# Sigmoid attention with a routed block: values with v as the stationary operand, four heads per step

## The chip, the core and the metric

The kernel runs on one core of a Trainium2 chip. The metric is the device time of one execution in microseconds. TensorE does the matmuls, VectorE and ScalarE the elementwise work, GpSimd the rest; SyncE (SP) and GpSimd issue the DMAs.

## The reference

Shapes: 8 batches, 12 heads, 448 tokens, 64 features per head, all float32; model width D = 12 x 64 = 768, hidden width 1024, capacity 128.

```
scores = q @ k.T / sqrt(64) - log(448)
attn   = 1 / (1 + exp(-scores))
x      = (attn @ v), heads side by side: (8, 448, 768)
per batch b:
  s   = x[b] @ w_gate                      # (448,)
  top = the 128 tokens with the largest s
  h   = relu(x[b, top] @ w1); ye = h @ w2
  out[b] = x[b]; out[b, top] += sigmoid(s[top])[:, None] * ye
```

## The kernel before, in words

Work goes by pairs of heads: 48 pairs, six per batch. `load` (L65 to L76) brings q, k and v of two pairs in three DMAs of 448 KB on the SP queue, tokens on 112 partitions, four consecutive tokens per partition, two loads ahead. `transposes` (L121) lets GpSimd put the two heads of a pair side by side (L128), turns the four 112-token chunks of q and of k on TensorE against an identity (L132) into a PSUM buffer of the pool `ps_1`, and VectorE copies them out (L137), so that the 64 features of each head lie on partitions.

`scores` (L140) makes one chunk of 112 keys for both heads: two matmuls of 64 rows, 448 query columns (L146), one head in partitions 0 to 63, the other in 64 to 127; ScalarE then takes one sigmoid over 896 elements per partition out of a `ps_sc` buffer (two of them) into the attention tile (L152). `values` (L157) makes 112 query rows of the output for both heads: for each head four matmuls that accumulate over the key chunks, with a 112x112 block of attention as the stationary operand and 64 columns of v streaming (L167). After the fourth chunk VectorE copies the pair's 112x512 result into x_b, the batch's 112x4x768 tile (L174).

The main loop (L303) interleaves by hand: for each chunk c, scores of pair i, then values of pair i - 1; after chunk 1 the transposes of pair i + 1; after chunks 1 and 3 one piece of the routed block of an earlier batch (`step`). The pieces of the routed block are: `store_and_gate` (x_b to out by one DMA on SP, the gate's dot products on VectorE, L187, a diagonal on GpSimd), `rank` (the gates of all tokens to all partitions by a matmul with ones, L200 and L202; VectorE counts for every token how many rank above it, L212, and builds one-hot columns, L218), `select` (eight narrow matmul passes per batch for index and gate, L226), `gather` (the 128 chosen rows, turned, as matmuls of x_b with the one-hot columns, L242), `ffn1` (two parts of 4 x 6 matmuls, L256, and a relu on ScalarE), `ffn2` (two parts of 8 matmuls of 384 columns, L268, times the gate on VectorE, L270), and `scatter` (an indirect DMA on GpSimd that adds the rows to out, L273). All PSUM tiles of the routed block and the transposes share the two `ps_1` buffers; x_b has two buffers. Each engine runs its instructions in program order, and the order above is the program order.

Of the kernel before, what the change touches and what calls it, by code (L numbers as in the profile page):

```python
# [16 lines left out]
def kernel(  # L17
# [17 lines left out]
    P = 128  # L35
    CP = 112            # tokens on the partitions: token p * NCH + c is row p of chunk c
    NCH = S // CP
    NPAIR = H // 2
    GP = 2              # head pairs per load
    NG = NPAIR // GP  # L40
# [3 lines left out]
    N = B * NPAIR  # L44
# [3 lines left out]
    PSUM = bass.MemoryType.PSUM  # L48
    assert S == NCH * CP and D == KD * P and F == KF * P and KF % 4 == 0 and 0 < CAP < S
# [4 lines left out]
    raw = ctx.enter_context(tc.tile_pool(name="raw", bufs=3))  # L54
# [8 lines left out]
    raws = {}  # L63

    def load(gi):  # L65
        b, g = divmod(gi, NG)
        h0, nh = 2 * GP * g, 2 * GP
        tiles = []
        for nm, src in (("q", q), ("k", k), ("v", v)):
            t = raw.tile([CP, nh, NCH, Dh], F32, name=f"raw_{nm}")  # L70
            nc.sync.dma_start(
                out=t.rearrange("p h c d -> p h (c d)"),
                in_=src[b, h0:h0 + nh].rearrange("h (p c) d -> p h (c d)", c=NCH),
            )
            tiles.append(t)
        raws[gi] = tiles  # L76
# [3 lines left out]

    iden = const.tile([P, P], F32, name="iden")
    make_identity(nc, iden)
    bias_s = const.tile([P, 1], F32, name="bias_s")
    nc.vector.memset(bias_s, NEG_LOG_S)

# [5 lines left out]
    # earlier[p, c, t]: 1 where position t of the row lies before token (c, p)  # L91
# [3 lines left out]
    # [..., 0] the token's number in its sequence, [..., 1] its gate score  # L95
    tok_gate = [const.tile([CP, NCH, 2], F32, name=f"tok_gate{n}") for n in range(2)]

    def late_consts():
# [5 lines left out]
        for w, src in ((w1_sb, moe_w1), (w2_sb, moe_w2)):  # L104
            nc.gpsimd.dma_start(out=w, in_=src.rearrange("(t p) f -> p t f", p=P))
# [4 lines left out]
        for t in tok_gate:  # L110
            nc.gpsimd.iota(t[:, :, 0], pattern=[[1, NCH]], base=0,
                           channel_multiplier=NCH, allow_small_or_imprecise_dtypes=True)
# [6 lines left out]
    qkT, attn = {}, {}  # L119

    def transposes(i):  # L121
        b, hp = divmod(i, NPAIR)
        g, gi = divmod(hp, GP)
        tiles = raws[b * NG + g]
        qkT[i] = head.tile([P, 2, NCH, CP], F32, name="qkT")
        for a in range(2):
            pairs = head.tile([CP, NCH, 2, Dh], F32, name=f"pairs{a}")
            nc.gpsimd.tensor_copy(  # L128
                pairs, tiles[a][:, 2 * gi:2 * gi + 2].rearrange("p j c d -> p c j d"))
            ptr = ps_1.tile([P, 512], F32, name="ps1")  # L130
            for c in range(NCH):
                nc.tensor.transpose(  # L132
                    ptr[:, c * CP:(c + 1) * CP],
                    pairs[:, c].rearrange("p j d -> p (j d)"),
                    iden[:CP, :CP],
                )
            nc.vector.tensor_copy(  # L137
                qkT[i][:, a], ptr[:, :S].rearrange("e (c p) -> e c p", c=NCH))

    def scores(i, c):  # L140
        t = qkT[i]
        if c == 0:
            attn[i] = head.tile([CP, 2, NCH, S], F32, name="attnT")
        psc = ps_sc.tile([P, 2, 512], F32, name="psc")
        for j in range(2):
            nc.tensor.matmul(  # L146
                psc[:CP, j, :S],
                t[j * Dh:(j + 1) * Dh, 1, c, :],
                t[j * Dh:(j + 1) * Dh, 0].rearrange("e c p -> e (c p)"),
                start=True, stop=True,  # L150
            )
        nc.scalar.activation(attn[i][:, :, c, :], psc[:CP, :, :S], AF.Sigmoid,  # L152
                             bias=bias_s[:CP], scale=QK_SCALE)

    x_tiles, pav = {}, {}

    def values(i, m):  # L157
        b, hp = divmod(i, NPAIR)
        g, gi = divmod(hp, GP)
        vt = raws[b * NG + g][2]  # L160
        if m == 0:
            pav[i] = ps_o.tile([P, NCH, 2, Dh], F32, name="pav")
            if hp == 0:
                x_tiles[b] = xp.tile([CP, NCH, D], F32, name="x_b")
        for j in range(2):
            for c in range(NCH):
                nc.tensor.matmul(  # L167
                    pav[i][:CP, m, j, :],
                    attn[i][:, j, c, m * CP:(m + 1) * CP],
                    vt[:, 2 * gi + j, c, :],  # L170
                    start=(c == 0), stop=(c == NCH - 1),
                )
        if m == NCH - 1:
            nc.vector.tensor_copy(  # L174
                x_tiles[b][:, :, 2 * hp * Dh:2 * (hp + 1) * Dh],
                pav.pop(i)[:CP].rearrange("p c j d -> p c (j d)"))
# [171 lines left out]
```

## Time and profile before

| | us |
|---|---|
| median of three runs | 848.65 |
| the three runs | 847.45, 848.65, 849.12 |
| span of the profiled execution, first to last instruction | 846.6 |
| TensorE (PE) busy in it | 815.3 |
| PE weight loads (PEld), beside PE | 610.0 |
| ScalarE busy | 205.3 |
| VectorE (DVE) busy | 195.5 |
| GpSimd (POOL) busy | 84.8 |

The profile is of one execution, on the only core. Busy times of engines overlap one another. A matmul's record contains its way through the array, so records of consecutive matmuls overlap, and the distance of their starts, or the chain of work that ended last, shows what one costs. Each fp32 matmul stands there as two weight loads and two MATMUL records.

### The profile page before, as it was taken

To read this page: it belongs to the slowest core of one execution; us is meant where nothing else is said; L and a number is where in the kernel's file an instruction comes from. 1 tells how busy PE (TensorE), PEld (TensorE's weight loads), DVE (VectorE), ACT (ScalarE), POOL (GpSimd) and SP (SyncE) were. 2 spreads that over 40 slices of the span, in tenths; PEclk is the share of its full clock that TensorE was granted. 3 is DMA by queue.
4 is the path that set the end of the run, shared out by engine and by line. 5 is a ranking of instruction groups with operands and counts; after the bars stand their busy time and mean duration, and the time that the engine had idled before them with its cause. 6 is when DMAs were issued, how large, how long until landed. Compare 5 with 4: busy or idle time off the path is not lost.

```text
span 846.6 us, 12702 instructions
## 1 busy us (share of the span) xinstructions
PE 815.3 (96%) x5728; PEld 610.0 (72%) x5728; DVE 195.5 (23%) x425; ACT 205.3 (24%) x217; POOL 84.8 (10%) x131
## 2 busy tenths in 40 slices
PE   6999999999999999999999999999999999999586
PEld 4677787677876778677786778767787677876484
DVE  0211601134101341113401143011611125101420
ACT  2433311232122321233121331213311232112000
POOL 5111100101001100011000110011100111000000
PEclk9999999999999999999899999999999999999778
DMA  9952310331003410124101232032320201001101
GB/s 279 314 120 60 107 48 1 85 115 60 23 1 84 130 45 23 42 43 131 44 22 44 41 132 66 1 63 54 102 65 1 41 11 77 2 1 19 65 1 19
DMA packets 37030, 54.64 MB, mean 65 GB/s; under 512 B 1456, under 2 KB 33712, under 8 KB 36080
## 3 DMA queue, kind: packets, MB, share of 16 engines
q1 hardware_dynamic: 34432, 44.05, 17.9%
q0 software_dynamic: 2544, 9.78, 4.9%
q8 instruction: 45, 0.74, 0.4%
q14 instruction: 9, 0.07, 0.0%
HBM read 39.67 MB, written 14.16 MB: 64 GB/s over the span
## 4 chain that ended last, share of the span: by engine, by line
PE 91%; issue 5%; DVE 2%; DMA 1%; ACT 0%; POOLq 0%; POOL 0%
PE pav L167 39%; PE psc L146 23%; PE ps L256 9%; PE ps L268 9%; PE ps L242 6%; PE ps L132 4%; PE ps L226 1%; DMA out_dram<-x_b 1%; PE ps L200 1%; DVE qkT L137 1%; DVE junk L212 1%; DMA raw_q<-in_q_dram 0%; ACT attnT L152 0%; DVE sel L218 0%; POOLq L343 0%
## 5 line engine op out<-in xcount | busy, mean ns | idle before, releaser
L167 PEld LDWEIGHTS pav<-raw_v,attnT 112*112 112x112 f32 x3072 | 317.5, 178 | 118.9 <-issue 118.3
L167 PE MATMUL pav<-raw_v,attnT 112*112 112x64 f32 x3072 | 345.4, 265 | 0.4 <-ACT attnT L152 0.4
L152 ACT ACTIVATE attnT<-psc,bias_s 112x896 f32<-112x896 f32 x192 | 193.1, 1007 | 467.2 <-PE psc L146 467.2
L146 PE MATMUL psc<-qkT 64*112 64x448 f32 x768 | 217.1, 589 | 1.0 <-DVE qkT L137 0.7
L137 DVE COPY qkT<-ps 128x448 f32<-128x448 f32 x96 | 56.2, 619 | 213.0 <-PE ps L132 213.0
L174 DVE COPY x_b<-pav 112x512 f32<-112x512 f32 x48 | 33.2, 692 | 261.5 <-PE pav L167 261.5
L256 PEld LDWEIGHTS ps<-xeT,w_sb 128*128 128x128 f32 x768 | 87.0, 192 | 4.8 <-DVE qkT L137 4.7
L256 PE MATMUL ps<-xeT,w_sb 128*128 128x128 f32 x768 | 89.5, 277 | 0.0
L268 PE MATMUL ps<-w_sb,hT 128*128 128x384 f32 x256 | 86.1, 490 | 0.0
L146 PEld LDWEIGHTS psc<-qkT 64*112 64x112 f32 x768 | 59.2, 173 | 30.7 <-issue 8.9
L128 POOL COPY pairs<-raw_q 112x512 f32<-112x512 f32 x48 | 29.5, 614 | 516.3 <-PE ps L132 449.9
L268 PEld LDWEIGHTS ps<-w_sb,hT 128*128 128x128 f32 x256 | 47.4, 190 | 34.6 <-DVE qkT L137 4.7
L242 PEld LDWEIGHTS ps<-sel,x_b 112*128 112x128 f32 x384 | 54.7, 232 | 5.9 <-issue 5.9
L242 PE MATMUL ps<-sel,x_b 112*128 112x128 f32 x384 | 56.4, 318 | 0.0
L132 PE MATMUL ps<-iden,pairs 112*128 112x112 f32 x384 | 47.8, 264 | 6.6 <-POOL pairs L128 6.0
L132 PEld LDWEIGHTS ps<-iden,pairs 112*128 112x128 f32 x384 | 40.0, 148 | 12.5 <-POOL pairs L128 7.1
L258 ACT ACTIVATE hT<-ps 128x512 f32<-128x512 f32 x16 | 9.6, 597 | 116.4 <-PE ps L256 116.4
L128 POOL COPY pairs<-raw_k 112x512 f32<-112x512 f32 x48 | 29.7, 619 | 15.5 <-DMA raw_k<-in_k_dram 9.4
L187 DVE CUSTOM_DVE_ANT_0 junk<-x_b,wg_b 112x768 f32<-112x768 f32 x32 | 30.6, 958 | 2.1 <-DVE x_b L174 0.5
L270 DVE TENSOR_SCALAR oe<-ps,gate 128x384 f32<-128x384 f32 x16 | 9.9, 618 | 90.9 <-PE ps L268 90.9
L273 POOL DMA_INDIRECT out_dram<-oe,idx x8 | 12.9, 1608 | 133.7 <-DVE oe L270 95.9
L245 DVE COPY xeT<-ps 128x384 f32<-128x384 f32 x16 | 8.9, 558 | 61.7 <-PE ps L242 61.7
(33 smaller groups left out, 121.8 us busy)
## 6 DMA issues: line engine op xcount, KB each, us to landing
raw_q<-in_q_dram SPq DMA_DIRECT2D x24, 448.0 KB, 4.0
raw_k<-in_k_dram SPq DMA_DIRECT2D x24, 448.0 KB, 4.9
raw_v<-in_v_dram SPq DMA_DIRECT2D x24, 448.0 KB, 3.9
out_dram<-x_b SPq DMA_DIRECT2D x8, 1344.0 KB, 6.6
w_sb<-in_moe_w_dram POOLq DMA_DIRECT2D x2, 3072.0 KB, 23.6
wg_b<-in_moe_w_gate_dram POOLq DMA_DIRECT2D x1, 336.0 KB, 6.7
out_dram<-oe,idx POOLq DMA_INDIRECT x8, 5.6
```

The source lines that it names most:

```text
L128: nc.gpsimd.tensor_copy(pairs, tiles[a][:, 2 * gi:2 * gi + 2].rearrange("p j c d -> p c j d"))
L132: nc.tensor.transpose(ptr[:, c * CP:(c + 1) * CP], pairs[:, c].rearrange("p j d -> p (j d)"), iden[:CP, :CP],)
L137: nc.vector.tensor_copy(qkT[i][:, a], ptr[:, :S].rearrange("e (c p) -> e c p", c=NCH))
L146: nc.tensor.matmul(psc[:CP, j, :S], t[j * Dh:(j + 1) * Dh, 1, c, :], t[j * Dh:(j + 1) * Dh, 0].rearrange("e c p -> e (c p)"), start=True, ...
L152: nc.scalar.activation(attn[i][:, :, c, :], psc[:CP, :, :S], AF.Sigmoid, bias=bias_s[:CP], scale=QK_SCALE)
L167: nc.tensor.matmul(pav[i][:CP, m, j, :], attn[i][:, j, c, m * CP:(m + 1) * CP], vt[:, 2 * gi + j, c, :], start=(c == 0), stop=(c == NCH - 1),)
L174: nc.vector.tensor_copy(x_tiles[b][:, :, 2 * hp * Dh:2 * (hp + 1) * Dh], pav.pop(i)[:CP].rearrange("p c j d -> p c (j d)"))
L187: nc.vector.tensor_tensor_reduce(out=junk, in0=x_b[:, c, :], in1=wg_b, scale=1.0, scalar=0.0, op0=ALU.mult, op1=ALU.add, accum_out=tg[:, c ...
L242: nc.tensor.matmul(ps[:, t - t0, :n], x_b[:, c, t * P:(t + 1) * P], sel[:, c, s0:s0 + n], start=(c == 0), stop=(c == NCH - 1))
L256: nc.tensor.matmul(ps[:, f, :n], w1_sb[:, t, fc * P:(fc + 1) * P], xeT[:, t, :n], start=(t == 0), stop=(t == KD - 1))
L268: nc.tensor.matmul(ps[:n, :ND], hT[:, t, :n], w2_sb[:, t, cols], start=(t == 0), stop=(t == KF - 1))
L273: nc.gpsimd.indirect_dma_start(out=out_flat[:, :], out_offset=bass.IndirectOffsetOnAxis(ap=st[b]["idx"][:n, 0:1], axis=0), in_=st[b]["oe"] ...
```

## The change

A step now holds four heads (24 steps, three per batch). What it does:

- `load`: q and k are read in eight DMAs of 32 partitions each, per tensor four: head of the pair (j) and half of the features (e) choose the partitions, token t x 14 + r is row r of partition t, and each partition reads one run of 864 floats (13 tokens of 64 and 32 floats) for two heads. v comes in four DMAs of 32 partitions with three tokens (768 bytes) per run, and the remaining half chunk in four DMAs with one token (256 bytes) per run. 16 DMAs per step, two steps ahead; q and k tiles have two buffers, v tiles three.
- `turn`: four VectorE 32x32 transposes per step (384, 384, 128 and 896 elements per lane) give kT and qT with features on partitions; the TensorE transposes and GpSimd copies of q and k are gone.
- `scores`: seven chunks per step: six of 128 keys for a pair of heads, and one that holds the half chunks (64 keys) of both pairs. One sigmoid each.
- `values`: v is stationary (64 columns), 448 columns of attention stream; the two heads of a pair write partitions 0 to 63 and 64 to 127 of one PSUM tile. First the half chunks (64 rows) of all four heads, then three chunks of 128. The result is x^T; VectorE copies it to xT, and `back` turns it with four TensorE transposes per pair into a `ps_1` buffer and copies that to x_b.
- `store_and_gate` stores x a second time, to a DRAM tile x_d; `select` fetches the 128 rows from x_d with an indirect DMA, and `turn_rows` turns them with six TensorE transposes per batch in two halves. The matmul `gather` is gone. `ffn2` adds the row, and `scatter` writes without addition.
- `ps_1` has one buffer, the layers have their own PSUM pool `ps_f` with one; x_b has one buffer.
- Order: in step i the chunks 0 to 3, slot 2i, the chunks 4 to 6, turn of step i + 1, loads of step i + 2, slot 2i + 1, values of step i. A slot holds first `back` (of step i - 1), then pieces of the routed block by a fixed table: for batch b, `store_and_gate` in slot 6b + 7, `rank` in 6b + 9, `select` in 6b + 11, `turn_rows` in 6b + 12 and 6b + 13, two of the eight `ffn1` pieces in each of 6b + 13 to 6b + 16, `ffn2` in 6b + 17 and 6b + 18, `scatter` in 6b + 18. The weights are loaded after the first four chunks of step 0. What remains after slot 47 runs behind the last step.

The diff's core:

```diff
-    xp = ctx.enter_context(tc.tile_pool(name="xp", bufs=2))
-    moe = ctx.enter_context(tc.tile_pool(name="moe", bufs=2))
+    moe = ctx.enter_context(tc.tile_pool(name="moe", bufs=1))
-    ps_1 = ctx.enter_context(tc.tile_pool(name="ps_1", bufs=2, space=PSUM))
+    ps_f = ctx.enter_context(tc.tile_pool(name="ps_f", bufs=1, space=PSUM))
+    ps_1 = ctx.enter_context(tc.tile_pool(name="ps_1", bufs=1, space=PSUM))
...
+            t = raw.tile([P, 2, TB * Dh], F32, name=f"raw_{nm}")
+            for j in range(2):
+                for e in range(2):
+                    p0 = (2 * j + e) * TT
+                    nc.sync.dma_start(
+                        out=t[p0:p0 + TT, :, 0:RUN],
+                        in_=bass.AP(
+                            tensor=src.tensor,
+                            offset=src.offset + (b * H + h0 + j) * S * Dh + e * TT,
+                            ap=[[TB * Dh, TT], [2 * S * Dh, 2], [1, RUN]]),
+                    )
...
+    def turn(i):
+        kT[i] = head.tile([P, 2, TB, TT], F32, name="kT")
+        src = raws[i][0].rearrange("p a (r d) -> p a r d", d=Dh)
+        for pr in range(2):
+            nc.vector.transpose(
+                kT[i][:, pr, :4 * NF],
+                src[:, pr, :4 * NF, 0:TT].rearrange("p (m c) d -> p c m d", c=NF))
+        nc.vector.transpose(kT[i][:, :, 4 * NF:], src[:, :, 4 * NF:, 0:TT])
+        qT[i] = head.tile([P, 2, TB, TT], F32, name="qT")
+        src = raws[i][1].rearrange("p a (r d) -> p a r d", d=Dh)
+        nc.vector.transpose(qT[i], src[:, :, :, 0:TT])
...
+        parts = [(pr, slice(4 * NF, TB), pr * Dh, Dh) for pr in range(2)]
+        if n < 2 * NF:
+            parts = [(n // NF, slice(4 * (n % NF), 4 * (n % NF) + 4), 0, P)]
+        for pr, rows, p0, np_ in parts:
+            for j in range(2):
+                d = slice(j * Dh, (j + 1) * Dh)
+                nc.tensor.matmul(
+                    psc[p0:p0 + np_, j, :S],
+                    kT[i][d, pr, rows, :].rearrange("e r t -> e (r t)"),
+                    qT[i][d, pr].rearrange("e r t -> e (r t)"),
+                    start=True, stop=True)
...
+    def values(i):
+        tv, th = raws[i][2:]
+        out_t = [ps_o.tile([P, S], F32, name="pav") for _ in range(2)]
+        for pr in range(2):
+            for j in range(2):
+                p = slice(pr * Dh, (pr + 1) * Dh)
+                nc.tensor.matmul(out_t[pr][j * Dh:(j + 1) * Dh], th[p, j, :],
+                                 attn[i][p, 2 * NF, j, :], start=True, stop=False)
+        xT[i] = head.tile([P, 2, S], F32, name="xT")
+        for pr in range(2):
+            for c in range(NF):
+                for j in range(2):
+                    nc.tensor.matmul(
+                        out_t[pr][j * Dh:(j + 1) * Dh],
+                        tv[:, 2 * pr + j, c * Dh:(c + 1) * Dh],
+                        attn[i][:, pr * NF + c, j, :],
+                        start=False, stop=(c == NF - 1))
             nc.vector.tensor_copy(
+                xT[i][:, pr].rearrange("p (t r) -> p r t", r=TB),
+                out_t[pr].rearrange("p (r t) -> p r t", t=TT))
...
+    def back(i, pr):
...
+        ps = ps_1.tile([P, NCH, P], F32, name="ps1")
+        for c in range(NCH):
+            nc.tensor.transpose(ps[:CP, c, :], xT[i][:, pr, c * CP:(c + 1) * CP], iden)
+        hp = 2 * g + pr
+        nc.vector.tensor_copy(x_tiles[b][:, :, hp * P:(hp + 1) * P], ps[:CP])
...
+        xe = moe.tile([P, D], F32, name="xe", bufs=2)
+        nc.gpsimd.indirect_dma_start(
+            out=xe[:n], out_offset=None, in_=st[b]["x_d"][:, :],
+            in_offset=bass.IndirectOffsetOnAxis(ap=row[:n, 0:1], axis=0))
...
+    def turn_rows(b, n, half):
+        if half == 0:
+            st[b]["xeT"] = moe.tile([P, KD, P], F32, name="xeT")
+        ps = ps_1.tile([P, 4, P], F32, name="ps1")
+        for t in range(3):
+            tt = half * 3 + t
+            nc.tensor.transpose(ps[:, t, :n], st[b]["xe"][:n, tt * P:(tt + 1) * P],
+                                iden[:n, :n])
+        nc.vector.tensor_copy(st[b]["xeT"][:, half * 3:half * 3 + 3, :n], ps[:, :3, :n])
...
+    for i in range(NI):
+        for n in range(NF + 1):
+            scores(i, n)
+        if i == 0:
+            load_weights()
+        fill(2 * i)
+        for n in range(NF + 1, 2 * NF + 1):
+            scores(i, n)
+        if i + 1 < NI:
+            turn(i + 1)
+        if i + 2 < NI:
+            load(i + 2)
+        fill(2 * i + 1)
+        values(i)
+    for s in range(2 * NI, last + 1):
+        fill(s)
```

## Rows read from the trace of the kernel before

**Rows 1.** The page's busy times: us, share of the span, instructions.

```profile
PE 815.3 (96%) x5728; PEld 610.0 (72%) x5728; DVE 195.5 (23%) x425; ACT 205.3 (24%) x217; POOL 84.8 (10%) x131
```

**Rows 2.** The page's chain that ended last: shares by engine, by line.

```profile
PE 91%; issue 5%; DVE 2%; DMA 1%; ACT 0%; POOLq 0%; POOL 0%
PE pav L167 39%; PE psc L146 23%; PE ps L256 9%; PE ps L268 9%; PE ps L242 6%; PE ps L132 4%; PE ps L226 1%; DMA out_dram<-x_b 1%; PE ps L200 1%; DVE qkT L137 1%; DVE junk L212 1%; DMA raw_q<-in_q_dram 0%; ACT attnT L152 0%; DVE sel L218 0%; POOLq L343 0%
```

**Rows 3.** Groups by line and shape: count, busy us, mean ns, idle before.

```profile
L167 PE MATMUL pav<-raw_v,attnT 112*112 112x64 f32 x3072 | 345.4, 265 | 0.4 <-ACT attnT L152 0.4
...
L152 ACT ACTIVATE attnT<-psc,bias_s 112x896 f32<-112x896 f32 x192 | 193.1, 1007 | 467.2 <-PE psc L146 467.2
...
L137 DVE COPY qkT<-ps 128x448 f32<-128x448 f32 x96 | 56.2, 619 | 213.0 <-PE ps L132 213.0
...
L174 DVE COPY x_b<-pav 112x512 f32<-112x512 f32 x48 | 33.2, 692 | 261.5 <-PE pav L167 261.5
```

**Rows 4.** Chain in order of time, 400 to 412 us: start, us, what.

```profile
400.85 0.79 PE ps L200 x2
...
401.75 0.94 PE psc L146 x4
402.69 1.72 PE pav L167 x16
...
407.06 0.41 PE ps L132 x4
```

**Rows 5.** Instructions of L146: shortest, median, longest duration in ns.

```profile
L146 PE MATMUL psc<-qkT x768: 536/627/1086, 8.7 to 783.8; 64*112 64x448 f32 x192
```

**Rows 6.** Waits: who for what, us in total, times, longest.

```profile
PEld pav L167 <- issue: 118.3, 178, 0.7
```

**Rows 7.** Timeline of ScalarE, 12.5 to 15.5 us: start, us, what, idle before.

```profile
13.34 1.91 ACT L152 ACTIVATE attnT<-psc,bias_s 112x896 f32<-112x896 f32 x2 [0.23 <-PE psc L146]
```

**Rows 8.** Timeline of all engines, 400.9 to 405.4 us.

```profile
404.33 1.01 PE L146 MATMUL psc<-qkT 64*112 64x448 f32 x4
...
405.39 1.01 ACT L152 ACTIVATE attnT<-psc,bias_s 112x896 f32<-112x896 f32 x1 [1.58 <-PE psc L146]
```

**Rows 9.** Timeline of the tail behind the last pair, 785 to 850 us.

```profile
800.35 0.40 PE L202 MATMUL ps<-tok_gate,iden 112*112 112x4 f32 x2
...
808.36 1.28 PE L226 MATMUL ps<-tok_gate,sel 112*128 112x2 f32 x6
...
817.35 11.13 PE L256 MATMUL ps<-xeT,w_sb 128*128 128x128 f32 x96
...
828.32 10.49 PE L268 MATMUL ps<-w_sb,hT 128*128 128x384 f32 x32
...
838.84 0.62 DVE L270 TENSOR_SCALAR oe<-ps,gate 128x384 f32<-128x384 f32 x1 [4.47 <-PE ps L268]
839.74 1.57 POOL L273 DMA_INDIRECT out_dram<-oe,idx  x1 [41.07 <-DVE oe L270]
```

**Rows 10.** Timeline of the start, 0 to 9.6 us.

```profile
0.75 0.38 SPq L71 DMA_DIRECT2D raw_q<-in_q_dram  x1
...
8.72 1.09 PE L146 MATMUL psc<-qkT 64*112 64x448 f32 x2 [0.72 <-DVE qkT L137]
```

**Rows 11.** DMA: the queue's packets, MB, share; issues: KB, us to landing.

```profile
q1 hardware_dynamic: 34432, 44.05, 17.9%
...
raw_q<-in_q_dram SPq DMA_DIRECT2D x24, 448.0 KB, 4.0
...
out_dram<-x_b SPq DMA_DIRECT2D x8, 1344.0 KB, 6.6
...
out_dram<-oe,idx POOLq DMA_INDIRECT x8, 5.6
```

**Rows 12.** Second 21.2 us: length, engines' busy us, granted clock, DMA share, GB/s.

```profile
21.20:42.40 21.20, 20.26 (x145) 13.14 (x143) 4.85 (x8) 8.85 (x9) 3.52 (x6) 1.00 1.07 313
```

More of the change, by code (lines that the diff above doesn't have):

```diff
@@ L140, in scores @@
[L140 to L176, printed above, removed]
+    def load_weights():
+        for w, src in ((w1_sb, moe_w1), (w2_sb, moe_w2)):
+            nc.gpsimd.dma_start(out=w, in_=src.rearrange("(t p) f -> p t f", p=P))
@@ L264, in ffn2 @@
         oe = st[b]["oe"]
-        ps = ps_1.tile([P, 512], F32, name="ps1")
+        ps = ps_f.tile([P, 512], F32, name="psf")
         cols = slice(part * ND, (part + 1) * ND)
@@ L275, in scatter, with put @@
             out_offset=bass.IndirectOffsetOnAxis(ap=st[b]["idx"][:n, 0:1], axis=0),
[L276 removed]
+            in_=st[b]["oe"][:n], in_offset=None)
+    places = {}
+    def put(s, fn, *args):
+        places.setdefault(s, []).append((fn, args))
     def routed(b):
[L279 to L280 removed]
+        s = 2 * NQ * (b + 1) + 1
+        put(s, store_and_gate, b)
+        put(s + 2, rank, b)
+        s += 4
         for s0, n in SLOTS:
[L282 to L288 removed]
@@ L291 @@
-    todo = []
-    def step():
-        while todo:
-            try:
-                next(todo[0])
-                return
-            except StopIteration:
-                todo.pop(0)
-    transposes(0)
-    late_consts()
-    for i in range(N + 1):
-        if i < N and i % GP == 0 and i // GP + 2 < B * NG:
-            load(i // GP + 2)
-        for c in range(NCH):
-            if i < N:
-                scores(i, c)
-            if i > 0:
-                values(i - 1, c)
-            if c == 1 and i + 1 < N:
-                transposes(i + 1)
-            if c % 2 == 1:
-                step()
-        if i > 0 and i % NPAIR == 0:
-            todo.append(routed(i // NPAIR - 1))
@@ L317 @@
-    while todo:
-        step()
+            put(s, select, b, s0, n)
+            for half in range(2):
+                put(s + 1 + half, turn_rows, b, n, half)
+            for f in range(KF):
+                put(s + 2 + f // 2, ffn1, b, n, f)
+            for part in range(2):
+                put(s + 2 + KF // 2 + part, ffn2, b, n, part)
+            put(s + 2 + KF // 2 + 1, scatter, b, n)
+            s += 2 + KF // 2 + 2
+    for i in range(NI):
+        put(2 * i + 2, back, i, 0)
+        put(2 * i + 3, back, i, 1)
@@ new lines, with fill @@
+    fills = {s: list(v) for s, v in places.items()}
+    places = {}
+    for b in range(B):
+        routed(b)
+    order = {}
+    last = max(places)
+    for s in range(last + 1):
+        own, rest = fills.get(s, []), places.get(s, [])
+        order[s] = own + rest
+    def fill(s):
+        for fn, args in order.get(s, []):
+            fn(*args)
+    turn(0)
+    late_consts()
+    for i in range(NI):
+        for n in range(NF + 1):
[11 more added lines that the diff above has]
+        values(i)
```

165 lines of the change are left out of this document (80 added, 85 removed).

## The prediction

> **What bounds the kernel now.** I read the busy times first: TensorE is busy 815.3 of 846.6 us, VectorE 195.5 [rows 1]. The chain that ended last says the same from the other side: 91% of it is PE work, 39% the values matmuls of L167, 23% the scores of L146, 9% each the two layers of the routed block, 6% its gather by matmul (L242), 4% the transposes of q and k (L132) [rows 2]. So time is won only where TensorE's own stream gets shorter, and lost where that stream begins to wait.
>
> The stream's unit is the pass: every fp32 matmul stands in the trace as two weight loads and two MATMULs (L167: 48 pairs x 4 chunks x 2 heads x 4 key chunks = 1536 matmuls, 3072 records [rows 3]). Sixteen values passes take 1.72 us [rows 4], 0.107 us each. They stream 64 columns but load 112 stationary columns each; that load is what they cost. The wider passes are set by what streams: 32 passes of 384 columns take 10.49 us [rows 9], 0.328 each, so 448 columns cost 0.328 x 448/384 = 0.38, and L200 has 0.79 for two [rows 4]. A score chunk is four passes of 448 columns, yet takes 0.94 [rows 4]: the two heads sit in different 64-row halves of the array and stream together, 2 x 0.38 = 0.76, and 0.18 is left over. Of that 0.09 is a weight load that nothing covers (passes last 627 or 536 ns [rows 5]); the rest is the change between the half-array and whole-array form, after which L167's loads stand idle 0.7 us, 178 times [rows 6].
>
> **The change, part by part**, for a step of four heads (24 steps; before, two pairs).
>
> *Values.* Before: 128 passes x 0.107 = 13.7 us. After, v is stationary (64 columns) and 448 columns of attention stream. Three full key chunks, two pairs, two heads, two passes: 24 passes, the two heads in the two column halves. If they stream together as the score halves do: 12 x 0.38 = 4.6. The half chunk uses four quarters of the array: 8 passes, 2 x 0.38 = 0.76 if all four overlap. Three changes of form at 0.1 (bounds 0.09 to 0.18 from above): 0.3. Sum 5.65. No row shows a column tile; the far bound is no overlap between the column halves, (24 + 4) x 0.38 + 0.3 = 10.9, the near one 5.65 less the switches, 5.35. I take 5.65, because L146 is the nearest row and its two halves overlap in full.
>
> *Scores.* Seven chunks for eight (the seventh in four quarters, 0.94 too), but in bursts of four and three with nothing between, on the same two PSUM buffers. A sigmoid starts 1.06 us after its chunk [rows 8], lasts 1.007 [rows 3] and two run 1.91 together, 0.905 apart [rows 7]. So the third chunk waits for the first sigmoid: it starts at 2.1, not 1.88, and the bursts cost 4.0 and 3.1, in sum 7.1. Bounds: 7 x 0.76 = 5.3 if PE alone set it, 7 x 1.06 = 7.4. Before it was 8 x 0.94 = 7.5. Almost nothing is won here.
>
> *Turning.* PE transposes of q and k go (16 passes a step, four in 0.41 [rows 4]), with GpSimd's copies and two VectorE copies per pair. Eight transposes bring x^T back: 2 x 0.41 and a change of form, 1.0. VectorE gets four 32x32 turns a step, 1792 elements per lane. No such instruction is in the trace; its copies take 619 ns for 448 elements and 692 for 512 [rows 3], 1.14 ns an element and 0.11 fixed, so 1792 x 1.14 + 4 x 0.11 = 2.5 us. I take that; they hide behind the second score burst and the values (3.1 + 5.65 = 8.8), so even 3.5 times the price costs nothing, and a price of zero gains nothing. VectorE in all: 2.5, two x^T copies 1.3, two x copies 1.4, a third of a batch's gate, rank and rest (some 15 us) 5: 10 us in a step of 14 to 23.
>
> *Routed block.* Its two layers stay: 11.13 and 10.49 a batch [rows 9]. Rank 0.9 stays, select is 8 small passes at 1.28/6 [rows 9], 1.7. The gather's 48 matmul passes go; in their place a row gather by DMA (unseen; bounds: a q load lands in 4.0 us, the scatter in 5.6 [rows 11], plus 1.57 on GpSimd [rows 9], so 4 to 7; I take 7, and one slot of 9 us or more covers it) and six transposes, 0.6. With one ps1 buffer where there were two, the second half of the turned rows follows x^T's transposes at once, and then the first layer waits for its copy: two copies and their hand-over, 1.8 a batch (0 if something hides it, 4 if the later halves wait as well). Batch: 26.6; a step: 8.9. The new token order, L270's added operand, the scatter without addition and the x^T copies (behind the first score burst, 4.0) stay beside TensorE's stream: nothing, except in the tail.
>
> *Loads.* q and k are read twice with overlap: 16 DMAs for 2.23 MB a step where three loads of 0.46 MB stood. SP's issue is 16 x 0.38 [rows 10] = 6 us, under a step. All traffic: 24 x 2.23 + two stores of x, 22.0 + gather and scatter 6.3 + weights 6.6 = 89 MB; at the 313 GB/s of the saturated second slice [rows 12] 284 us, hidden behind anything near 580. At the start three loads and the weights queue up, 13 MB or 42 us at that rate, while the third step's rows are wanted from 34 on: I take 3 us of waiting (0 to 10).
>
> *New waits.* x_b has one buffer: VectorE's first copy of a batch waits for the two stores of the last (each 6.6 us alone [rows 11], so 13), with the next step's turn and copies queued behind it and the scores behind those. It comes some 13 us after the stores are issued (two layer pieces, values, four score chunks), so 0, up to 4 a batch. On SP the store waits for the previous scatter, with later loads behind it; they run two steps ahead. On GpSimd the gather waits for VectorE, with the scatter and the next diagonal behind it, also slots ahead.
>
> **The sum.** Step with routed work: 7.1 + 1.0 + 5.65 + 8.9 = 22.65. Without (the first six: batch 0's layers begin in step 6): 7.1 + 1.0 + 5.65 and 0.7 for the last sigmoid, which nothing covers: 14.45. Start: scores began at 8.72 [rows 10], but q and k are now 1.77 MB where 0.92 stood (2.7 us more at 313 GB/s), so 12. Tail, from the end of the last values: x^T back 1.3, half of batch 5's second layer 5.25, turned rows 3.2, batch 6's layers with rank and select of batch 7 between them 11.1 + 10.5 + 0.9 + 1.7, the last gather's uncovered rest 2, its rows 2.4, batch 7's layers 11.1 + 0.8 + 10.5, VectorE 0.8, and the 7.1 from the end of L270 (839.46) to the end [rows 9]: 68.6. Together 12 + 6 x 14.45 + 18 x 22.65 + 68.6 + 3 = 578 of span. The median of the runs, 848.65, lies 2.0 above the profiled span; so 580.
>
> Two places of the Trainium skill speak against the change. TensorEngine Tiling (Array Packing), Key Properties, says that changing the tiling mode drains the engine; rows 6 agree, and the new step alternates among four forms; I priced this from the score chunk above. TensorE: Matmul & The Clock Gate, Measured speedup vs the span model, gives 2.38 times for three column tiles, so 0.79 of full overlap; by an estimate from that page the values cost 1.4 us more a step, and the time would be 614. No run here shows it yet.
>
> **The rivals.**
> *Partial overlap of the column tiles.* Each pair of passes pays a weight load of 0.09, as the first pass of a score chunk does [rows 5]: 14 x 0.09 x 24 = 30, so 610. For it: short stationary loads into two halves. Against: the second score passes hide theirs.
> *No overlap.* Column halves take turns, so the column tiling does nothing: 10.9 - 5.65 = 5.3 a step, 24 x 5.3 = 127, so 707. For it: no instruction of the trace writes PSUM from a column offset. Against: row halves overlap fully in the same fp32 form.
> *New waits bind.* Single buffers (ps1, x_b, psf) and in-order VectorE: 3 to 5 us a step in the 18 full steps, 634 to 670. For it: one buffer stands where two stood, and VectorE's rank block, 8 us from the rank's matmuls to the select's (800.35 to 808.36 [rows 9]), stands ahead of the x^T copies. Against: they come after the turn, with 8 us of matmuls behind them.
> *Slower: the loads bind.* Each q or k DMA fills only 32 partitions, v comes in 768-byte and 256-byte pieces. If the rate falls with the partitions reached, 313/4 = 78 GB/s, the 89 MB take 1140 us and TensorE waits in every step. It decides below 89 MB / 848 us = 105 GB/s. For it: no load of the trace is narrower than 112 partitions. Against: four such DMAs in flight reach all 128, and the queue's packets average 70 ns for 1.3 KB (17.9% of 16 x 846.6 us over 34432 [rows 11]), smaller than most of the new pieces. At half rate (156 GB/s, 570 us) it would just about hide.
>
> **How the numbers follow.** Forecast 580, chance 0.57, own range 540 (scores by PE alone, no waits) to 610; partial overlap 0.12; new waits 0.14; no overlap 0.12; loads bind 0.04; no change by some offsetting mixture 0.01. The range 540 to 690 holds the first three, 0.83. A measurement here can tell about 0.2% from no change; faster by that 0.955, within it 0.005, slower 0.04.
>
> **What would show it.** Values right: a stretch of 12 pairs of passes in about 4.6 us, starts in twos; wrong: starts 0.38 apart. Scores: sigmoids 0.9 to 1.1 apart in a burst, PE waiting for ACT. Turns: VectorE near 0.6 us for 384 elements, and no PE wait on them. Loads: no PE or VectorE wait on raw tiles after 50 us. Tail: about 69 us after the last values. The forecast is wrong if PE's idle time exceeds some 60 us or a values step exceeds 7 us.

## The result, and the profile after

The changed kernel takes 752.82 us (median of four runs, 751.88 to 755.67), 0.888 of the kernel before (95% interval 0.886 to 0.890). The forecast was 580 with a range of 540 to 690: the direction was right, the time lies outside the range. The profiled execution has a span of 750.1 us where the working gave 578, so 172 us are to be explained: the start took 4.9 us more than forecast, steps 0 to 5 57.9, the 18 full steps 103.3 and the tail 9.0, less the 3 counted for the loads.

The page of the changed kernel: busy times, the granted clock in 40 slices, the chain's shares, and the groups of the values, the turns of x^T and the turns of k (out<-in, count, busy us, mean ns, idle before and its releaser).

```profile
PE 571.5 (76%) x2896; PEld 295.0 (39%) x2896; DVE 229.3 (31%) x481; ACT 174.0 (23%) x193; POOL 31.2 (4%) x43
PEclk9889899869997799959999699987999689995999
PE 58%; DMA 13%; ACT 11%; DVE 10%; issue 6%; SPq 2%; POOLq 0%; DVEq 0%; ACTq 0%
...
L200 PE MATMUL pav<-attnT,raw_v 128*64 128x448 f32 x576 | 124.5, 551 | 0.0
...
L219 PE MATMUL ps<-iden,xT 128*112 128x128 f32 x192 | 37.8, 329 | 22.7 <-DVE x_b L221 12.0
...
L161 DVE STREAM_TRANSPOSE kT<-raw_k 128x384 f32<-128x384 f32 x48 | 25.2, 553 | 34.7 <-DMA raw_k<-in_k_dram 34.7
```

Where [rows 1] had TensorE busy for 815.3 of 846.6 us, it is busy for 571.5 of 750.1 now: it stands idle 178.6 us, 31.3 before. [rows 2] was PE for 91%; the chain is now 58% PE, and DMA, ScalarE and VectorE set the end for a third of the span. The matmul work itself shrank as planned. A step with little else in it, TensorE's timeline (start, us, operation, count, idle before it and its releaser):

```profile
341.36 1.77 PE L180 MATMUL psc<-qT,kT 64*128 64x448 f32 x8
343.55 1.92 PE L180 MATMUL psc<-qT,kT 64*128 64x448 f32 x8 [0.42 <-ACT attnT L185]
345.68 1.92 PE L180 MATMUL psc<-qT,kT 64*128 64x448 f32 x8 [0.21 <-ACT attnT L185]
347.81 0.98 PE L180 MATMUL psc<-qT,kT 64*64 64x448 f32 x8 [0.21 <-ACT attnT L185]
348.72 1.38 PE L306 MATMUL psf<-xeT,w_sb 128*128 128x128 f32 x10
350.03 0.98 PE L194 MATMUL pav<-attnT,raw_h 64*64 64x448 f32 x8
350.94 4.73 PE L200 MATMUL pav<-attnT,raw_v 128*64 128x448 f32 x24
355.60 0.65 PE L219 MATMUL ps<-iden,xT 128*112 128x128 f32 x4
```

The 24 passes of the full chunks take 4.73 us (the forecast had 4.6), the half chunk 0.91 from start to start, the seven score chunks 7.4 (7.1). So the column halves overlap in full. What went wrong lies between such stretches: what TensorE waited for, in sum (us, times, longest).

```profile
PE ps L274 <- DVE sel L265: 43.0, 7, 6.4
PE psc L180 <- DVE qT L167: 29.8, 6, 16.9
PE ps L294 <- DMA xe<-x_d,row: 22.0, 7, 3.3
PE psc L180 <- ACT attnT L185: 18.2, 66, 0.4
```

The select (L274) waits up to 6.4 us in each of seven batches, the turned rows (L294) up to 3.3: the two steps of the routed block that the code spreads over slots 11 and 12 of a batch, to lie beside matmuls. The timeline of one batch shows how little lies beside them:

```profile
404.65 1.01 PE L247 MATMUL ps<-diag,ones 112*112 112x448 f32 x2
...
408.79 0.65 PE L219 MATMUL ps<-iden,xT 128*112 128x128 f32 x4 [1.55 <-DVE x_b L221]
415.83 1.84 PE L274 MATMUL ps<-tok_gate,sel 112*128 112x2 f32 x8 [6.38 <-DVE sel L265]
418.25 1.10 PE L219 MATMUL ps<-iden,xT 128*112 128x128 f32 x4 [0.58 <-ACT gate L281]
422.53 0.87 PE L294 MATMUL ps<-iden,xe 128*128 128x128 f32 x3 [3.18 <-DMA xe<-x_d,row]
```

Two windows of the same batch, ahead of the wait and behind it (us, PE busy and instructions, PEclk, DMA share, GB/s):

```profile
396.00:404.00 8.00, 6.72 (x40) 1.00 0.01 2
415.00:420.00 5.00, 2.94 (x12) 0.50 0.78 178
```

The rank matmul (L247), written for slot 9, runs at 404.65; the select, written two slots later, is the next thing of its kind at 415.83, and between them stand one values matmul and transposes of x^T. TensorE waits for VectorE's whole rank block, then for the gather, and when it comes back four transposes take 1.10 us instead of 0.65 (408.79): the granted clock was 1.00 ahead of the wait and is 0.50 behind it. A batch takes 88.6 us (the first scores of its steps start 24.3, 24.0 and 40.2 us apart in the timeline), where the forecast had 68.

The section on the kernel before said that the order of the code is the program order. That is wrong. A planner that builds the program sets the order of each engine's instructions. TensorE's stream of the built program in such a batch (a matmul has two records in the trace and is counted once here, a transpose has one), against that of an experiment below that keeps the code's order:

```
changed kernel                                in the order of the code
L200 pav<-attnT,raw_v x7                      L248 ps<-diag,ones  (rank)
L219 ps<-iden,xT x4                           L250 ps<-tok_gate,iden
L200 pav<-attnT,raw_v x4                      L195 pav<-attnT,raw_h x4
L247 ps<-diag,ones  (rank)                    L201 pav<-attnT,raw_v x12
L249 ps<-tok_gate,iden                        L181 psc<-qT,kT x8
L200 pav<-attnT,raw_v                         L220 ps<-iden,xT x4
L219 ps<-iden,xT x4                           L307 psf<-xeT,w_sb x12
L219 ps<-iden,xT x4                           L181 psc<-qT,kT x8
L274 ps<-tok_gate,sel x4  (select)            L220 ps<-iden,xT x4
L219 ps<-iden,xT x4                           L320 psf<-w_sb,hT x8
L294 ps<-iden,xe x3  (turned rows)            L275 ps<-tok_gate,sel x4  (select)
```

On the right 52 wide matmuls and eight transposes stand between rank and select; on the left one and eight.

The other losses stand at the start: first scores at 16.9 us, not 12, and steps 0 to 5 together 144.6 us, not 86.7. Two rows of GpSimd's timeline show one reason:

```profile
4.88 0.91 POOL L150 DMA_DIRECT2D w_sb<-in_moe_w_dram  x1
7.82 0.93 POOL L150 DMA_DIRECT2D w_sb<-in_moe_w_dram  x1
```

The weights, written behind the first four score chunks, are issued at 4.88 and 7.82 us, and share the DMA engines with the loads of q, k and v of the first steps: VectorE's turn of k waits for its rows 34.7 us in three steps (L161 of the first fence). GpSimd does not wait for the score chunks here, so a place behind them in the code did not hold the weight loads back. The weights are the smaller part of what steps 0 to 5 lost: with TensorE alone in the code's order (below) and the weights issued as early, these steps take 113.6 us, so 31.0 of the 57.9 us are the order's.

### The profile page after: what moved, and what is told of

Same layout as the page of the kernel before. It is cut to its first block, busy times and chain, and to the rows that moved or that the text cites. A ratio compares the mean times of both kernels' runs of the same rounds, so it can differ in the third digit from the quotient of the medians.

```text
span 750.1 us, 7353 instructions
## 1 busy us (share of the span) xinstructions
PE 571.5 (76%) x2896; PEld 295.0 (39%) x2896; DVE 229.3 (31%) x481; ACT 174.0 (23%) x193; POOL 31.2 (4%) x43
## 4 chain that ended last, share of the span: by engine, by line
PE 58%; DMA 13%; ACT 11%; DVE 10%; issue 6%; SPq 2%; POOLq 0%; DVEq 0%; ACTq 0%
PE pav L200 14%; PE psf L306 12%; PE psc L180 12%; PE psf L319 10%; ACT attnT L185 10%; DMA raw_q<-in_q_dram 5%; DMA xe<-x_d,row 4%; DVE junk L259 3%; PE ps L219 3%; PE pav L194 3%; DMA raw_h<-in_v_dram 2%; PE ps L274 2%; SPq L81 2%; PE ps L294 1%; DVE x_b L221 1%
## 5 line engine op out<-in xcount | busy, mean ns | idle before, releaser
L185 ACT ACTIVATE attnT<-psc,bias_s 128x896 f32<-128x896 f32 x168 | 161.8, 1004 | 292.3 <-PE psc L180 292.0
L180 PE MATMUL psc<-qT,kT 64*128 64x448 f32 (+1 forms) x768 | 165.6, 597 | 48.3 <-DVE qT L167 29.8
L200 PE MATMUL pav<-attnT,raw_v 128*64 128x448 f32 x576 | 124.5, 551 | 0.0
L205 DVE COPY xT<-pav 128x448 f32<-128x448 f32 x48 | 44.2, 923 | 243.1 <-PE pav L200 243.1
L180 PEld LDWEIGHTS psc<-qT,kT 64*128 64x128 f32 (+1 forms) x768 | 53.5, 180 | 151.1 <-ACT attnT L185 101.3
L306 PE MATMUL psf<-xeT,w_sb 128*128 128x128 f32 x768 | 104.6, 297 | 9.4 <-ACT hT L309 4.9
L306 PEld LDWEIGHTS psf<-xeT,w_sb 128*128 128x128 f32 x768 | 99.0, 210 | 18.6 <-DVE xeT L296 7.5
L319 PE MATMUL psf<-w_sb,hT 128*128 128x384 f32 x256 | 90.1, 497 | 10.9 <-ACT hT L309 5.5
L200 PEld LDWEIGHTS pav<-attnT,raw_v 128*64 128x64 f32 x576 | 40.3, 138 | 72.5 <-issue 69.6
L319 PEld LDWEIGHTS psf<-w_sb,hT 128*128 128x128 f32 x256 | 46.3, 189 | 51.7 <-DVE oe L321 9.7
L274 PE MATMUL ps<-tok_gate,sel 112*128 112x2 f32 x64 | 13.8, 338 | 43.0 <-DVE sel L265 43.0
L194 PE MATMUL pav<-attnT,raw_h 64*64 64x448 f32 x192 | 26.4, 568 | 15.9 <-ACT attnT L185 13.5
L161 DVE STREAM_TRANSPOSE kT<-raw_k 128x384 f32<-128x384 f32 x48 | 25.2, 553 | 34.7 <-DMA raw_k<-in_k_dram 34.7
L274 PEld LDWEIGHTS ps<-tok_gate,sel 112*128 112x128 f32 x64 | 13.5, 311 | 45.3 <-issue 45.0
L294 PE MATMUL ps<-iden,xe 128*128 128x128 f32 x48 | 13.1, 407 | 22.9 <-DMA xe<-x_d,row 22.0
## 6 DMA issues: line engine op xcount, KB each, us to landing
x_d<-x_b SPq DMA_DIRECT2D x8, 1344.0 KB, 11.3
```

Source lines behind the costliest of these rows:

```text
L161: nc.vector.transpose(kT[i][:, pr, :4 * NF], src[:, pr, :4 * NF, 0:TT].rearrange("p (m c) d -> p c m d", c=NF))
L180: nc.tensor.matmul(psc[p0:p0 + np_, j, :S], kT[i][d, pr, rows, :].rearrange("e r t -> e (r t)"), qT[i][d, pr].rearrange("e r t -> e (r t)" ...
L185: nc.scalar.activation(attn[i][:, n], psc[:, :, :S], AF.Sigmoid, bias=bias_s, scale=QK_SCALE)
L194: nc.tensor.matmul(out_t[pr][j * Dh:(j + 1) * Dh], th[p, j, :], attn[i][p, 2 * NF, j, :], start=True, stop=False)
L200: nc.tensor.matmul(out_t[pr][j * Dh:(j + 1) * Dh], tv[:, 2 * pr + j, c * Dh:(c + 1) * Dh], attn[i][:, pr * NF + c, j, :], start=False, sto ...
L205: nc.vector.tensor_copy(xT[i][:, pr].rearrange("p (t r) -> p r t", r=TB), out_t[pr].rearrange("p (r t) -> p r t", t=TT))
```

## The experiments

Times are medians; ratios are to the kernel before, run beside each. Line numbers shift by one to three where lines were added.

**Two x_b buffers, nothing else.**

```diff
-            x_tiles[b] = moe.tile([CP, NCH, D], F32, name="x_b")
+            x_tiles[b] = moe.tile([CP, NCH, D], F32, name="x_b", bufs=2)
```

> The changed kernel with two buffers for x_b instead of one; nothing else. In the changed kernel's trace a batch takes 88.6 us (select at 327.2 to select at 415.8) where the prediction had 3 x 22.65 = 68, and TensorE stands 6.4 us before the select and 3.2 us before the turned rows in every batch, because the rank's matmuls stand only 11 us ahead of the select's in TensorE's stream. Theory A (the knot): x_b's single buffer holds the x^T copies back, and with them the rank behind them, until rank, select and gather follow each other directly. Then two buffers put the rank some 15 us ahead of the select, the 6.4 us and the low clock after it go, 9 to 12 us a batch, 680 to 700 us in all. Theory B (the loads bind: 16 narrow DMAs a step): nothing changes, 740 to 755. Theory C (both): 700 to 735.

Measured: 685.86 us (0.809, interval 0.807 to 0.810), within theory A's range. What TensorE waited for:

```profile
PE psc L180 <- DVE qT L167: 40.8, 12, 16.9
...
PE ps L274 <- DVE x_b L221: 5.5, 7, 0.8
```

The select's 43 us of waiting for VectorE's rank are gone (5.5 are left, for a copy), and the turn of q is now the costliest wait. A batch takes some 79 us. A second buffer wins 67 us here, and the planner, given two, made another order, with the select 24.5 us behind the rank (345.84 to 370.37) where it stood 11.2 behind; how much of the 67 is the wait for the buffer and how much the order, this run can't tell.

**TensorE held in the order of the code.** Every matmul and transpose is tied to the one written before it; x_b keeps one buffer.

```diff
+    keep = tc.keep_in_program_order
...
-                nc.tensor.matmul(
+                keep(nc.tensor.matmul(
```

> The changed kernel with TensorE's instructions held in the order in which they are written (an issue-order edge from each to the one before, no wait); all other engines as planned, one x_b buffer. Theory A (the order that the planner made for TensorE costs the 20 us a batch): 18 full steps return to 22.65 to 24 us each, 625 to 660 in all, with the select's and the turned rows' waits gone. Theory B (the loads bind): TensorE now waits for the turns of q and k instead, 720 to 760. If the single x_b buffer binds in the written order (two stores of 6.4 and 11.3 us before the next batch's first x copy), a wait of 5 us a batch at the x^T transposes remains: 660 to 690.

Measured: 591.38 us (0.697, interval 0.694 to 0.699), better than expected by more than 30 us. No instruction was taken away and no buffer added. TensorE's waits:

```profile
PE psc L181 <- DVE qT L168: 31.1, 5, 17.5
PE psc L181 <- ACT attnT L186: 17.6, 48, 0.4
PE ps L295 <- DVE x_b L222: 6.3, 8, 0.8
```

The waits of the select (but for 0.8 us) and for the gathered rows are gone; a batch takes 66.4 us (forecast 68.0), the tail 66.1 (68.6). The order is the cause of the larger part: 161 of the 172 us. That the loads bind falls with it, since all transfers are still there.

**The same with two x_b buffers.**

> As the run with TensorE in the written order, and two buffers for x_b. Theory A: 620 to 650, the difference to the run with one buffer being what x_b's buffer costs in the written order (0 to 5 us a batch). Theory B: as with one buffer, 720 to 760.

Measured: 646.61 us (0.763), 55 us slower than with one buffer. The time lies in theory A's range, but not for its reason: by theory A the second buffer wins 0 to 5 us a batch, and it lost. TensorE waits for VectorE's turn of q 19 times, 16.5 of the 69.2 us at the start:

```profile
PE psc L181 <- DVE qT L168: 69.2, 19, 16.5
```

VectorE's and TensorE's timelines around one such wait:

```profile
326.64 0.69 DVE L260 SCALAR_TENSOR_TENSOR junk<-rep,ones_row 112x448 f32<-112x448 f32 x1
...
332.37 0.69 DVE L260 SCALAR_TENSOR_TENSOR junk<-rep,earlier 112x448 f32<-112x448 f32 x1
...
333.79 1.10 DVE L168 STREAM_TRANSPOSE qT<-raw_q 128x896 f32<-128x896 f32 x1
...
326.78 4.73 PE L201 MATMUL pav<-attnT,raw_v 128*64 128x448 f32 x24
334.94 1.77 PE L181 MATMUL psc<-qT,kT 64*128 64x448 f32 x8 [3.43 <-DVE qT L168]
```

The comparisons of the rank (L260) stand ahead of the turn that the next scores need; in the code they stand behind it. VectorE's order is planned too, and with a second buffer it came out so that TensorE waits at most steps. A freed resource made the kernel slower through the order that it allowed.

**No loads after the second step, the planner's order.**

```diff
     def load(i):
+        if i >= 2:
+            raws[i] = raws[i - 2]
+            return
```

> The changed kernel without the loads of steps 2 to 23: these steps use the tiles of steps 0 and 1 again, so 22 of 24 loads are left out and the attention of later steps is of other data; all the arithmetic stays. With no loads to wait for, the planner's order for TensorE is nearly the written one. Theory A (order): time falls as in the runs with the order held, 610 to 640, less the start's excess of some 30 us. Theory B (the transfers themselves bind): the same fall here, but none where the order is held with the loads in place. So this run prices the loads; the comparison with the held order tells the theories apart.

Measured: 588.70 us (0.693), as theory A had it (580 to 610 with the start's excess taken off). A batch takes 66.9 us, as much as with all loads and TensorE held (66.4). In the steady state the transfers thus cost nothing on the chip. They cost what the planner makes of them: without them its order comes close to the code's (the select stands 22.5 us behind the rank, as with TensorE held). Why the planner, with the loads in, chooses the order that it does, wasn't looked into.

**TensorE and VectorE held, one x_b buffer.** As above, with every VectorE instruction tied as well.

> TensorE and VectorE both held in the written order, one x_b buffer. In the run with TensorE alone held, the turn of q stands behind the x^T copies on VectorE and TensorE waits 2.0 us for it at each of steps 3 to 5. Theory A (order is the cause on VectorE too): these waits go, 578 to 588. Theory B (the loads are what the turn waits for): the same 2 us stay and VectorE's later work queues behind the waiting turn, 590 to 610.

Measured: 588.35 us (0.695), 0.4 us above theory A's range, and the waits of 2.0 us are gone. Steps 2 and 3, which hold only attention, take 14.5 us each, the forecast's 14.45. Step 4 takes 24.3; VectorE's longest wait in it:

```profile
DVE x_b L222 <- DMA x_d<-x_b: 10.5, 1, 10.5
```

This is the wait that the prediction named (copy into the one x_b behind the stores, the turn behind it), and it binds in the first batch alone. The store to x_d lands no later there than in the others (11.5 us, the median). But SP, with the loads ahead of it in its queue, issues the stores 5.1 us behind the batch's last copy (81.8 to 86.9 us), and step 4 has no layer pieces that would put the next copy off. In batch 1 the stores go out at 139.3 us, right behind the copy, and the next copy comes at 153.0, after the landing.

**TensorE and VectorE held, two x_b buffers.**

> As the run with both engines held, with two x_b buffers. With TensorE alone held the second buffer made the kernel slower, 646.6 against 591.4, and TensorE waited 69 us for the turn of q in 19 places. Theory A: that loss came through VectorE's planned order (the turn behind the gate's and the rank's blocks), not through the buffer; with VectorE held too the two kernels are equal within 3 us, 578 to 590. Rival: the second buffer costs by itself (x stored while the next is written, more DMA at once): still 630 to 650.

Measured: 579.80 us (0.685, interval 0.683 to 0.687), span 577.7. Against the same with one buffer it gains 8.5 us, which is step 4's wait; held, the second buffer costs nothing, so the 55 us above were VectorE's order (theory A). TensorE by stretch (start, steps 0 to 5, 18 full steps, tail; columns as in the windows above), here and in the changed kernel:

```profile
0.00:16.70 16.70, 0.00 (x0) 1.00 0.89 217
16.70:119.80 103.10, 84.96 (x438) 0.95 0.96 234
119.80:511.90 392.10, 372.72 (x2159) 1.00 0.57 145
511.90:577.70 65.80, 54.08 (x306) 0.99 0.20 67
sum 577.70, PE 511.76; mean PE 127.94
```

```profile
0.00:16.90 16.90, 0.01 (x1) 1.00 0.90 235
16.90:161.50 144.60, 103.98 (x474) 0.86 0.70 172
161.50:672.50 511.00, 411.15 (x2120) 0.91 0.43 109
672.50:750.10 77.60, 56.34 (x305) 0.86 0.17 56
sum 750.10, PE 571.48; mean PE 142.87
```

The first fence is the held kernel, the second the changed one. Of the 172.4 us between them 112.7 are idle time (750.1 - 571.5 = 178.6 against 577.7 - 511.8 = 65.9) and 59.7 are longer busy time of the same 2896 records: in the full steps the granted clock was 0.91 against 1.00.

**TensorE and VectorE held, one x_b, weights held back to steps 2 and 4.** A one-column write ties each weight load to VectorE's order.

```diff
-    def load_weights():
-        for w, src in ((w1_sb, moe_w1), (w2_sb, moe_w2)):
-            nc.gpsimd.dma_start(out=w, in_=src.rearrange("(t p) f -> p t f", p=P))
+    def load_weights(n):
+        w, src = ((w1_sb, moe_w1), (w2_sb, moe_w2))[n]
+        keep(nc.vector.memset(w[:, 0, 0:1], 0.0))
+        nc.gpsimd.dma_start(out=w, in_=src.rearrange("(t p) f -> p t f", p=P))
...
-        if i == 0:
-            load_weights()
+        if i in (2, 4):
+            load_weights(i // 2 - 1)
```

> Both engines held, and the two weight loads (6.3 MB) made to wait for steps 2 and 4 by a one-column write on VectorE, where the planner had put them at 5 and 8 us from the start. Theory: they share the DMA engines with the first loads, so that step 0 starts at 17 us instead of 12 and takes 28 us instead of 14.5; held back, step 0 starts at 12 to 14 and takes 16 to 19, and steps 2 to 5 pay up to 2 us each: 560 to 572, some 15 us under the run without. Rival: the start is bound by the number of DMAs in flight (each of the 16 waits for an older one's landing), not by the weights: 575 to 588, no gain.

Measured: 584.65 us (0.689); the expected 560 to 572 was missed, and the time lies in the rival's range, though its reason fails: step 0 did gain. Step 0 takes 16.2 us instead of 26.9, as expected, and step 4 takes 35.3 instead of 24.3. VectorE's longest wait there:

```profile
DVE x_b L223 <- DMA x_d<-x_b: 20.4, 1, 20.4
```

The second weight load now runs beside the stores that the one x_b waits for. Almost all of the gain was given back.

**The three together** (both held, two x_b, weights in steps 2 and 4).

> The three repairs together: TensorE and VectorE held in the written order, x_b in two buffers, the two weight loads held back to steps 2 and 4 by a one-column VectorE write. Theory (three separate causes that add up): with the weights late the first scores start near 14.6 us and step 0 takes 16 us, where with the weights early it was 16.7 and 26.4; steps 1 to 5 take 14.5 to 15.8 each, since with two x_b buffers no copy waits for the stores in step 4 as it did with one (35.3 us); the rest as with early weights (18 full steps, tail 65.8). Expected 579.8 - 2 - 10 - 1.5 = 566, range 562 to 571. Rival (the start only moves its wait: the weights, loaded in steps 2 to 5, take the load rate of those steps, and TensorE waits there for what it no longer waits for at the start): 576 to 582, no gain over the version with early weights.

Measured: 575.61 us (0.679, interval 0.677 to 0.680): between the two ranges, 0.4 us from the rival's. First scores at 14.5 us, step 0 in 15.9, steps 1 to 4 in 14.5 to 15.8, as the theory had it; but step 5 takes 25.5. Three of the DMA issues between 60 and 120 us (KB, median us to landing):

```profile
w_sb<-in_moe_w_dram POOLq DMA_DIRECT2D x1, 3072.0 KB, 15.4
out_dram<-x_b SPq DMA_DIRECT2D x1, 1344.0 KB, 14.0
x_d<-x_b SPq DMA_DIRECT2D x1, 1344.0 KB, 16.8
```

Weights and both stores are in flight together (the stores land in 6.4 and 11.3 us otherwise, by the page of the changed kernel), the next k comes 5.0 us late for VectorE's turn, with it the copies behind the turn, and TensorE's select waits 7.5 us. So the wait moved: the rival's mechanism, at most of its price.

**Weights in steps 1 and 2, and in steps 2 and 6**, all else as in the last. Only the two step numbers change.

> As the version with everything (both engines held, two x_b buffers, weights late, 575.6 us), but the two weight loads go out in steps 1 and 2 where they went out in steps 2 and 4. In that version step 5 took 25.5 us, 10 more than the 15.7 with the weights at the start: the second weight load ran beside the two stores of batch 0 (14.0 and 16.8 us to landing), k of the next step came 5.0 and q 2.4 us too late for VectorE's turns, and TensorE's select waited 7.5 us for the copy behind them. Theory (it was the meeting of weights and stores; the stores begin in step 3): with the weights in steps 1 and 2 they meet nothing but the loads, which run two steps ahead; step 5 takes 15.7, time 575.6 - 8 = 567, range 564 to 570. Rival (3 MB of weights beside the loads of any step of 14.5 us is too much, 2.2 + 3.1 MB at some 313 GB/s being 17 us): the wait moves to step 2 or 3 and the time stays at 573 to 580.

> The same with the weight loads in steps 2 and 6, so that the second meets the stores of batch 1 and not those of batch 0, in a step that takes 19 us and not 14.5. Theory (weights and stores meet): 2.2 + 3.1 + 2.75 MB in step 6, 8.1 MB, is some 20 to 26 us at 313 to 400 GB/s, so the loads fall behind by up to 5 us, which two steps of lead take up or not: 567 to 575. If the stores don't matter at all and only the short step did, 567.

Measured: 575.19 us (0.678) for steps 1 and 2, the rival's time, though the wait moved to steps 4 and 5 (18.5 and 22.9 us) and not to 2 or 3. For steps 2 and 6, 570.08 us (0.671, interval 0.670 to 0.672), within the theory's range; step 5 takes 21.4, and step 6, which has the weights now, 19.4 as ever. So meeting the stores is only part of it: with no weights there at all step 5 still loses 3.8 us at the select. In the first six steps the DMA engines are nearly always busy, with both weight loads at the start (share 0.96, 234 GB/s) and with one of the two moved out to step 6 (0.95, 223); in step 6, of some 20 us, the weights cost no time. This is the fastest version: 24% below the changed kernel, without one arithmetic instruction fewer.

**The kernel before, TensorE held in the order of its code.**

> The kernel before with its TensorE stream held in the written order, nothing else changed. It tells whether the planner's reordering is a cost of any kernel here or of the changed one alone. Theory (the planner's order hurts where it bunches work of unequal waits around single buffers; before, TensorE idled only 23.5 us in all, so no more than that is to be won): 825 to 850, ratio 0.97 to 1.0. Rival (holding the written order by itself is worth much on TensorE, whatever the kernel, some 20% as on the changed kernel): below 800. A third outcome, slower than before by 1% or more, would say that in the kernel before the planner filled waits that the written order leaves open.

Measured: 853.11 us (1.005, interval 1.003 to 1.007), between the first and the third outcome. Its longest sums of waits:

```profile
PE ps L227 <- DVE sel L219: 14.6, 8, 6.6
PE ps L133 <- POOL pairs L129: 8.0, 3, 5.6
```

In the planner's order these two sums are 9.1 and 6.0 us. In the kernel before the planner's order is worth 4 us, not a loss. So holding an order is no gain in itself: the reordering that was harmless there cost 161 us in the changed kernel.

## Why the prediction was wrong

**The step that failed** is the assumption under the sum, not a term of it: that each engine runs the code's order. From it came "slot" as a cover: the gather behind "one slot of 9 us or more", the select behind VectorE's rank, the tail's order. These waits were put at nothing; in the changed kernel the select waited 43.0 us and the turned rows 22.0, and a batch took 88.6 us where the sum had 68.0. The prediction's own sign of being wrong showed: TensorE idle above some 60 us, measured 178.6. The trace of before shows it, in a stretch that the prediction read for durations only (TensorE's timeline):

```profile
409.28 0.38 PE L226 MATMUL ps<-tok_gate,sel 112*128 112x2 f32 x2 [0.36 <-DVE sel L218]
409.53 0.58 PE L167 MATMUL pav<-raw_v,attnT 112*112 112x64 f32 x4
409.95 0.34 PE L226 MATMUL ps<-tok_gate,sel 112*128 112x2 f32 x2
410.14 0.39 PE L167 MATMUL pav<-raw_v,attnT 112*112 112x64 f32 x2
```

The code issues the passes of the select (L226) in one piece; here they stand among values passes. With the order held on two engines, the kernel that the prediction priced takes 588.35 us, and with a second x_b 579.80.

**That this equals 580 is in part luck.** The 579.80 has a buffer that the forecast did not have, and by stretch, forecast against that held kernel, errors cancel: start 12 and 16.7; steps 0 to 5 86.7 and 103.1; loads 3, contained in those two; the 18 full steps 407.7 and 392.1; tail 68.6 and 65.8. The first six steps and the start were 18 too cheap with the loads counted (119.8 against 101.7), the rest 18 too dear.

**Values: right.** 5.65 forecast; 0.91 + 4.66 from start to start. No overlap and partial overlap fall. The Trainium skill (TensorE: Matmul & The Clock Gate, Measured speedup vs the span model) would have made it 614 by an estimate; 24 passes in 4.73 us speak against carrying its 2.38 of 3 over to two tiles of 64 columns.

**Change of form: right in size.** The eight half-chunk passes take 0.91 us from start to start where two times 0.38 stream: 0.15 is left over, within the 0.09 to 0.18 taken. The Trainium skill's drain at a change of mode (TensorEngine Tiling (Array Packing), Key Properties) is no larger than that here.

**Scores: right** where both bursts have something between: 4.0 and 3.1 forecast, 4.04 and 3.05 with TensorE held (303.65 to 307.69 and 310.95 to 314.00 us); and 7.4 in the changed kernel, which makes all seven chunks at a stretch (the far bound).

**Turns on VectorE: right.** 553 ns for 384 elements (0.55 by the estimate), 1.10 us for 896. From step 2 on they hid when VectorE's order was held (25.5 us of waits in all, in two places, both at the start); with VectorE's order left to the planner and two x_b buffers they cost 69.2 us. The two x^T copies were mis-sized, 1.3 us a step forecast and 1.85 measured (923 ns each), beside TensorE's stream.

**Routed block: a little too dear.** A batch takes 66.0 us held, 68.0 forecast; the select 0.95 instead of 1.7 (the row that it was priced from stands in a stretch where the granted clock was 0.50, and it was 1.00 here), the wait between the halves of the turned rows 0.8 instead of 1.8. The gathered rows land 4.3 us after their issue, 7 taken.

**Loads: right in the steady state, wrong at the start.** Taking them out changes a batch by 0.5 us. But 3 us of waiting (0 to 10) for the start was too little: to the end of step 5 it took 18 us more than the 98.7 + 3 forecast with the weights early (119.8), and 8.5 more with the weights in steps 2 and 6 (110.2). The rate of the saturated slice [rows 12] was used, and the weights were in the 13 MB; not counted was that the loads of the steps behind the third and batch 0's stores fall into the same first 100 us.

**New waits.** The rival at 634 to 670 had in-order VectorE and single buffers in it. The one x_b buffer binds in one step only (10.5 us, where 0 to 4 a batch were taken) while the order is held; ps1 costs 0.8 a batch. The rival's price was passed in the planner's order: of the 67 us between one buffer and two there, 8.5 remain with the order held. Nor is the single buffer all of it: with two buffers the planner's order still takes 685.86 us, 106 more than the held one.

## What to carry to other kernels

Before a schedule is priced, compare the order in the trace with the order in the code; where a planner stands between them, every cover that the sum counts on has to be found in the trace, or be held by explicit order. Freeing a buffer is not safely a gain while the order is open: the same edit won 67, lost 55 and won 8.5 us here, depending on which engines were held. And in the first steps price the DMA as one account, since a load that is put off meets the stores of what it was put off behind.

## What the runs showed of the hardware

Two tiles of 64 stationary columns in fp32 stream fully together: 24 passes of 448 columns in 4.73 us, 0.39 a pair, the price of one pass in L200 of before [rows 4]. VectorE's 32x32 turn of fp32 costs what a copy costs: 553 ns for 384 elements, where a copy of 384 (xeT, L296) takes 557, and 1.10 us for 896.

The clock makes a wait dearer than its length. In the timeline above TensorE stood idle for 6.38 us, the granted clock fell from 1.00 to 0.50 (2.4 to 1.2 GHz), and four transposes took 1.10 us instead of 0.65. How much of the 59.7 us of extra busy time is the clock and how much the other order of forms wasn't separated.
